# A gated attention and SwiGLU kernel: the product of VectorE's masked key tiles moved to GpSimd

## The chip, the cores and the metric

The kernel runs on one core of one Trainium2 chip. The metric is the device time of one execution in microseconds (us). Before the change it is 769.66 us, the median of three runs (769.5 to 769.75).

The engines of a core work side by side, each on its own queue of instructions in order: TensorE (PE) multiplies matrices into PSUM, ScalarE (ACT) evaluates functions such as the exponential, VectorE (DVE) does elementwise work, GpSimd (POOL) can do elementwise work in SBUF too, and SyncE (SP) starts transfers.

## The reference

An attention block and a SwiGLU block read the same 2048 rows of `x`, and a per-row gate mixes their outputs (bf16; D = 512, 32 heads of 16, F = 1792):

```python
x = A_x
g = sigmoid((x * gate_w).sum(-1, keepdims=True))
q, k, v = split(x @ A_wqkv)                      # 32 heads of 16
p = softmax(einsum("bhqd,bhkd->bhqk", q, k) * 16 ** -0.5)
a = merge(einsum("bhqk,bhkd->bhqd", p, v)) @ A_wo
b = (silu(x @ B_w_gate) * (x @ B_w_up)) @ B_w_down
return g * a + (1 - g) * b
```

The bulk of the elementwise work is the exponential of 32 x 2048 x 2048 scores.

## The kernel before

The scores are computed with keys on the partitions. A *unit* is one block of 512 queries with one group of four heads; there are 4 x 8 = 32 units. A *key tile* is 128 keys of one unit: four heads of 512 queries, so 128x2048 scores. Each unit has 16 key tiles, 512 in all. TensorE makes the scores of a tile (`score`), an engine makes the exponentials in bf16, and TensorE multiplies them with the values and a column of ones (`pv`, accumulating in `o_ps`), one pass of four matmuls for each 128x2048 tile of weights.

Two engines share the exponentials. ScalarE takes the key tiles of a unit from the front, 1024 columns an instruction, from the PSUM tiles `s_t` to `e_all`. VectorE takes tiles from the back of a unit (`v_take`), from PSUM tiles `d_t`, one bank of 512 columns an instruction, and builds an approximation of the exponential out of bit patterns: four evictions (`first` in `emit_d`, line 862) write `y`, a scaled score as a 16-bit integer that read as bf16 is a rough power of two. It then goes on in one of two ways, chosen by `quad` and kept in `groups[n]`:

- four copies (`copy`, line 887): `y` itself and three operations of 128x2048, SBUF to SBUF, that add a constant to the integer; TensorE sums all four, so the tile costs four value passes;
- two copies (`bits` and `product`, lines 895 and 904): one mask keeps the mantissa bits of `y` (line 898), a second keeps sign and exponent (line 901), and a product of `y` and the mantissa mask, read as bf16, makes the second term (line 906). This is two 128x2048 masks and one two-input 128x2048 operation on VectorE, and two value passes.

The results `c_t` lie in six buffers of 128x2048 and a seventh place, which is first a part of `wd_t` and later a part of `kaug`; at most three tiles `y` are in work at a time (`NY`). The feed-forward matmuls, projections and output are cut into pieces that fill TensorE's gaps, and their evictions also go through VectorE. The three PSUM banks of the `m` pools hold `d_t` as well as the pieces.

The order of the instructions on each engine is fixed when the program is built. `ordered` (line 156) chains the instructions of one engine in the order in which the code makes them, so in the profile all VectorE work has the line of that helper, L180, TensorE's L168 and ScalarE's L171. A planner (`Plan`) keeps a clock for each engine, `plan.pe`, `plan.act` and `plan.dve`, adds a fixed price for every instruction, and picks what comes next by these clocks: `fill_dve` orders VectorE's evictions (`d_wait`), masks, copies and products (`vops`) and other work (`owed`); `pv_list` lists the passes whose input is ready by the plan; `v_unit` lets VectorE take another tile if it would be done `LEAD` (in the last unit `LAST`) before ScalarE reaches the end of the unit. On the chip an instruction waits for its inputs by semaphores, but never overtakes the one ahead of it on its engine.

GpSimd only fills constants at the start.

## Time and profile before

| | us |
|---|---|
| median of three runs | 769.66 (769.5 to 769.75) |
| profiled execution | 768.54 |
| its span, first to last instruction | 766.8 |
| TensorE matmul busy | 740.6 (97%) |
| ScalarE busy | 750.8 (98%) |
| VectorE busy | 734.6 (96%) |
| GpSimd busy | 10.6 (1%) |
| granted TensorE clock | 0.999 |

The page of the profile lists the busy time of each engine over the span. The table by stage gives the same for stretches of the span. A group collects the instructions of one engine with the same operation and operands: after the bar come their busy time together, the mean length of one in ns, and the idle time ahead of them with what ended it. In the order of time each row has its start, its length and, in brackets, idle time ahead of it. Lengths are from dispatch to completion, so consecutive rows on one engine can overlap a little; what one more instruction costs is read from start to start.

### The profile page before, as it was taken

To read this page: it belongs to the slowest core of one execution; us is meant where nothing else is said; L and a number is where in the kernel's file an instruction comes from. 1 tells how busy PE (TensorE), PEld (TensorE's weight loads), DVE (VectorE), ACT (ScalarE), POOL (GpSimd) and SP (SyncE) were. 2 spreads that over 40 slices of the span, in tenths; PEclk is the share of its full clock that TensorE was granted. 3 is DMA by queue.
4 is the path that set the end of the run, shared out by engine and by line. 5 is a ranking of instruction groups with operands and counts; after the bars stand their busy time and mean duration, and the time that the engine had idled before them with its cause. 6 is when DMAs were issued, how large, how long until landed. Compare 5 with 4: busy or idle time off the path is not lost.

```text
span 766.8 us, 24169 instructions
## 1 busy us (share of the span) xinstructions
PE 740.6 (97%) x10109; PEld 246.0 (32%) x10109; DVE 734.6 (96%) x1234; ACT 750.8 (98%) x843; POOL 10.6 (1%) x25
## 2 busy tenths in 40 slices
PE   8999999999999999999999999999999999999997
PEld 3333333333333233333333333323333333333332
DVE  7899999999999999999999999999999999999993
ACT  6999999999999999999999999999999999999996
POOL 5000000000000000000000000000000000000000
PEclk9999999999999999999999999999999999999999
DMA  9000313144210013211200130212000232100001
GB/s 222 6 2 15 67 21 78 34 117 87 62 28 13 17 41 78 58 33 28 51 18 24 32 95 21 69 28 56 12 19 17 69 80 56 31 18 7 22 30 35
DMA packets 91029, 34.53 MB, mean 45 GB/s; under 512 B 75488, under 2 KB 90472, under 8 KB 90920
## 3 DMA queue, kind: packets, MB, share of 16 engines
q1 hardware_dynamic: 89192, 32.66, 17.7%
q8 instruction: 79, 1.29, 0.7%
q10 hardware_dynamic: 1728, 0.33, 0.2%
q14 instruction: 30, 0.25, 0.1%
HBM read 21.55 MB, written 2.35 MB: 31 GB/s over the span
## 4 chain that ended last, share of the span: by engine, by line
ACT 48%; PE 27%; DVE 13%; issue 11%; DMA 0%; DVEq 0%; ACTq 0%
ACT e_all L171 45%; DVE c_t L180 9%; PE s_t L168 9%; PE o_ps L168 8%; PE gu L168 5%; ACT th L171 2%; PE dps L168 2%; DVE kaug L180 1%; PE qp L168 1%; DVE mt L180 1%; PE vp L168 1%; PE warm L168 1%; DVE gs L180 1%; DVE osb L180 1%; PE kp L168 0%
## 5 line engine op out<-in xcount | busy, mean ns | idle before, releaser
L171 ACT ACTIVATE e_all<-s_t 128x1024 bf16<-128x1024 f32 x774 | 722.9, 1049 | 3.2 <-PE s_t L168 1.6
L180 DVE TENSOR_SCALAR c_t<-d_t 128x512 uint16<-128x512 f32 x432 | 285.8, 681 | 4.8 <-PE d_t L168 4.5
L168 PE MATMUL s_t<-qx,kaug 32*128 32x512 bf16 (+1 forms) x1224 | 237.6, 385 | 11.6 <-ACT e_all L171 10.2
L168 PE MATMUL o_ps<-e_all,vaug 128*32 128x512 bf16 (+3 forms) x2024 | 170.1, 334 | 0.8 <-ACT e_all L171 0.6
L168 PEld LDWEIGHTS <-kaug 32*128 32x128 bf16 (+1 forms) x2048 | 80.6, 91 | 275.8 <-issue 268.6
L180 DVE TENSOR_SCALAR c_t<-c_t 128x2048 uint16<-128x2048 uint16 x236 | 157.7, 682 | 0.4
L168 PE MATMUL d_t<-qx,kaug 32*128 32x512 bf16 x408 | 153.2, 384 | 0.3 <-DVE qx L180 0.3
L168 PEld LDWEIGHTS <-vaug 128*32 128x32 bf16 x4112 | 101.9, 95 | 131.8 <-issue 94.7
L168 PE MATMUL o_ps<-c_t,vaug 128*32 128x512 bf16 (+3 forms) x1768 | 136.3, 341 | 0.7 <-DVE osb L180 0.6
L168 PE MATMUL gu<-xT,wg 128*32 128x512 bf16 x896 | 71.9, 383 | 0.1
L168 PE MATMUL gu<-xT,wu 128*32 128x512 bf16 x896 | 70.2, 383 | 0.0
L168 PE MATMUL ops<-wd_t,mt 128*32 128x512 bf16 x672 | 58.1, 382 | 0.0
L180 DVE TENSOR_SCALAR kaug<-d_t 128x512 uint16<-128x512 f32 x60 | 40.0, 682 | 0.9 <-PE d_t L168 0.7
L180 DVE SCALAR_TENSOR_TENSOR mt<-gs,gu 128x512 bf16<-128x512 bf16 x56 | 38.1, 680 | 1.6
L180 DVE TENSOR_TENSOR c_t<-c_t 128x2048 bf16<-128x2048 bf16 x32 | 38.8, 1214 | 0.0
L168 PE MATMUL s_t<-q,kaug 32*128 32x512 bf16 (+1 forms) x188 | 36.4, 385 | 2.4 <-ACT e_all L171 2.2
L180 DVE SCALAR_TENSOR_TENSOR gs<-th,gu 128x512 bf16<-128x512 bf16 x56 | 38.0, 678 | 0.1
L171 ACT ACTIVATE th<-gu 128x512 bf16<-128x512 f32 x56 | 35.0, 624 | 0.0
L168 PEld LDWEIGHTS <-mt 128*32 128x32 bf16 (+1 forms) x1037 | 25.0, 95 | 26.2 <-issue 19.6
L180 DVE TENSOR_SCALAR kaug<-c_t 128x2048 uint16<-128x2048 uint16 x46 | 31.3, 680 | 0.0
L180 DVE TENSOR_SCALAR c_t<-kaug 128x2048 uint16<-128x2048 uint16 x42 | 28.1, 683 | 0.0
L168 PEld LDWEIGHTS <-wg 128*32 128x32 bf16 x896 | 18.1, 94 | 25.3 <-issue 21.3
(142 smaller groups left out, 434.1 us busy)
## 6 DMA issues: line engine op xcount, KB each, us to landing
wg<-in_B_w_gate_dram SPq DMA_DIRECT2D x56, 128.0 KB
wu<-in_B_w_up_dram SPq DMA_DIRECT2D x56, 128.0 KB
on<-osb SPq DMA_DIRECT2D x120, 16.0 KB
rb<-rr SPq DMA_DIRECT2D x15, 128.0 KB
wd_t<-in_B_w_down_dram SPq DMA_DIRECT2D x7, 256.0 KB
qx<-qst SPq DMA_DIRECT2D x96, 16.0 KB
qx<-aq SPq DMA_DIRECT2D x96, 16.0 KB
out_dram<-o_t SPq DMA_DIRECT2D x12, 128.0 KB
```

What stands on the lines that cost most here:

```text
L168: return ordered(nc.tensor.matmul(*args, **kw))
L171: ordered(nc.scalar.activation(*args, **kw))
L180: return lambda *a, **kw: ordered(f(*a, **kw))
```

## The change

When VectorE takes a key tile, the planner now asks whether GpSimd has room: the tiles assigned to it and not yet finished by VectorE's masks, at 4.7 us each (`POOL_US`), plus what `plan.pool` is ahead of `plan.dve`, must be below 9 us (`POOL_AHEAD`). If so, the tile takes the two-copy form, and its product is issued on GpSimd instead of VectorE, right after the mantissa mask. The mask of sign and exponent stays on VectorE. If not, `quad` decides as before; in the built program all 38 other tiles of VectorE come out with the four-copy form, so none is left for `product`. A tile for GpSimd keeps its buffer of `y` until both the second mask and the product are done. `LEAD` goes from 8 to 11 us and `LAST` from 6 to 10, and in the count of ScalarE's tiles left the present one is subtracted whole, begun or not. The built program has 94 products on GpSimd; 40 products on VectorE are gone.

```diff
+    gps = Ordered(nc.gpsimd)
...
     class Plan:
-        pe = dve = act = 0.0
+        pe = dve = act = pool = 0.0
...
+    POOL_US, POOL_PE, POOL_AHEAD = 4.7, 0.15, 9
...
             if groups[n] == 2:
-                vops.extend([(0.6, lambda: bits(n, 0, y), ("y", n), n, True), (0.6, lambda: bits(n, 1, y), None, n, True),
-                             (MUL_US, lambda: product(n, h, y), None, n, False)])
+                vops.extend([(0.6, lambda: bits(n, 0, y, h), ("y", n), n, True), (0.6, lambda: bits(n, 1, y, h), None, n, True)])
+                if n in by_pool:
+                    users[h][0] = 2
+                else:
+                    vops.append((MUL_US, lambda: product(n, h, y), None, n, False))
...
+    by_pool = set()
+
+    def bits(n, k, y, i):
         h, c = home()
         if k == 0:
             vec.tensor_scalar(out=c, in0=y, scalar1=0x007F, scalar2=0x3F00, op0=ALU.bitwise_and, op1=ALU.bitwise_or)
             part[n] = (h, c)
+            if n in by_pool:
+                h, c = part.pop(n)
+                gps.tensor_tensor(out=c.bitcast(BF16), in0=y.bitcast(BF16), in1=c.bitcast(BF16), op=ALU.mult)
+                plan.pool = max(plan.pool, plan.dve + 0.1) + POOL_US
+                copies[n, 1] = (c.bitcast(BF16), h)
+                vready.append((plan.pool + POOL_PE, n, 1))
+                drop(i, plan.pool + POOL_PE)
+                y_live[0] -= 1
         else:
+            if n in by_pool:
+                by_pool.remove(n)
+                drop(i, plan.dve + 0.05)
             vec.tensor_scalar(out=c, in0=y, scalar1=0xFF80, scalar2=None, op0=ALU.bitwise_and)
             ready(n, 0, h, c)
...
-    LEAD, LAST = 8.0, 6.0
+    LEAD, LAST = 11.0, 10.0
...
-            left = hi[vu] - (at_ + begun if vu == au else 0)
+            left = hi[vu] - (at_ + 1 if vu == au else 0)
...
-        groups[n] = 2 if quad() else 4
+        if len(by_pool) * POOL_US + max(0.0, plan.pool - plan.dve) < POOL_AHEAD:
+            by_pool.add(n)
+            groups[n] = 2
+        else:
+            groups[n] = 2 if quad() else 4
```

More of the change, by code (lines that the diff above doesn't have):

```diff
@@ L893, in copy @@
             y_live[0] -= 1
-    def bits(n, k, y):
+    by_pool = set()
+    def bits(n, k, y, i):
         h, c = home()
```

## The prediction

> **What bounds the kernel now.** I read the page's busy line first, then the table by stage, then the order of time on VectorE, then the start, the only stretch where GpSimd works.

> ```profile
> PE 740.6 (97%) x10109; PEld 246.0 (32%) x10109; DVE 734.6 (96%) x1234; ACT 750.8 (98%) x843; POOL 10.6 (1%) x25
> ```

> Three engines are full and GpSimd is empty. The table by stage (columns: stretch, its length, busy time and count of TensorE, weight load, VectorE, ScalarE, GpSimd, clock, DMA share, GB/s) shows that this holds nearly to the end:

> ```profile
> 0.00:20.00 20.00, 16.79 (x163) 6.98 (x167) 14.12 (x41) 12.61 (x16) 10.61 (x25) 1.00 0.88 214
> 384.00:480.00 96.00, 93.62 (x1264) 30.71 (x1260) 95.92 (x156) 95.99 (x108) 0.00 (x0) 1.00 0.15 38
> 740.00:767.00 27.00, 22.02 (x275) 8.01 (x273) 13.58 (x25) 20.61 (x24) 0.00 (x0) 0.97 0.08 25
> ```

> Between 20 and 740 us neither ScalarE nor VectorE has more than about 3 us in 96 free. So a gain needs less work on ScalarE, and a loss on VectorE shows in full, but for the little it had free. VectorE's order of time shows what it does (start, length, instruction):

> ```profile
> 400.26 0.68 DVE L180 TENSOR_SCALAR kaug<-c_t 128x2048 uint16<-128x2048 uint16 x1
> 400.86 1.28 DVE L180 TENSOR_SCALAR c_t<-d_t 128x512 uint16<-128x512 f32 x2
> 402.06 1.21 DVE L180 TENSOR_TENSOR c_t<-c_t 128x2048 bf16<-128x2048 bf16 x1
> 403.19 0.68 DVE L180 TENSOR_SCALAR c_t<-d_t 128x512 uint16<-128x512 f32 x1
> ```

> Instructions overlap by about 0.08, so from start to start a 512-column eviction out of PSUM costs 0.60 us, a 2048-column operation inside SBUF also 0.60, and the 2048-column product 1.13. The groups carry the counts (mean length in ns after the comma):

> ```profile
> L171 ACT ACTIVATE e_all<-s_t 128x1024 bf16<-128x1024 f32 x774 | 722.9, 1049 | 3.2 <-PE s_t L168 1.6
> L180 DVE TENSOR_SCALAR c_t<-d_t 128x512 uint16<-128x512 f32 x432 | 285.8, 681 | 4.8 <-PE d_t L168 4.5
> L180 DVE TENSOR_SCALAR c_t<-c_t 128x2048 uint16<-128x2048 uint16 x236 | 157.7, 682 | 0.4
> L180 DVE TENSOR_TENSOR c_t<-c_t 128x2048 bf16<-128x2048 bf16 x32 | 38.8, 1214 | 0.0
> ```

> No row has GpSimd reading two tensors. Its nearest rows are fills:

> ```profile
> L254 POOL MEMSET kaug<- 128x1024 f32 x3 | 2.7, 957 | 0.0
> L522 POOL MEMSET qx<- 128x2048 bf16 x1 | 1.8, 1810 | 0.1
> ```

> 1810 ns for 2048 bf16, 957 for 1024 f32: about 0.9 ns per element and column, whatever its width.

> **The change, part by part.** The counts after are from the listing of the changed program's instructions; durations are the rows above.

> *Tiles and ScalarE.* VectorE's key tiles rise from 125 to 132 (evictions 500 to 528, four each). Seven tiles leave ScalarE: 774 exponentials become 760. Five in a row take 4.72 us of which the last takes its full 1.05, so one costs 0.92 from start to start: 14 x 0.92 = 12.9 us less.

> *TensorE.* 94 VectorE tiles now take the two-copy form (before 40), 38 the four-copy form (before 85). Value passes: before 85x4 + 40x2 + 387 of ScalarE's = 807, after 38x4 + 94x2 + 380 = 720. A second pass adds 0.22 us (0.62 for eight matmuls against 0.40 for four): 19 us less. This lies beside ScalarE; it only means TensorE does not become the bound.

> *VectorE.* 40 products go: -40 x 1.13 = -45.2. SBUF-to-SBUF operations of 2048 columns fall from 335 to 302: -33 x 0.60 = -19.8. Evictions: +28 x 0.60 = +16.8. Sum -48.2; its 734.6 busy become 686.4.

> *GpSimd.* 94 products on an empty queue; the fills of the start are ahead of the first and nothing is behind one but the next. Price of one, from the fill's 0.88 ns per element: one pass over 2048 columns is 1.81, two passes (the two reads) 3.62, three (and the write) 5.43. I take the middle of the last two, 4.5, since both operands must at least be read; 94 x 4.5 = 423 us, so it keeps up. [...]

> *What the product does to VectorE.* This is the term that decides. The fast VectorE forms read SBUF at one rate: 2048 elements in 0.60 us with one input, 4096 in 1.13 with two, 3.4 and 3.6 per ns, against 0.85 out of PSUM. That looks like a read path filled to its limit in both forms. If GpSimd's reads go over part of the same path, the two cannot run together. Lower bound of the cost: nothing (a path of its own). Upper bound: whoever starts first holds the path for its whole instruction. The start shows no collision, but only between writers: VectorE's first fill here runs beside a long GpSimd fill, its second when GpSimd has ended, and both take 0.91.

> ```profile
> 2.65 2.28 POOL L270 MEMSET vaug<- 128x512 bf16 x1
> 3.26 0.91 DVE L254 MEMSET kaug<- 128x1024 f32 x1 [0.16 <-issue]
> ...
> 13.46 0.91 DVE L180 MEMSET kaug<- 128x1024 f32 x1 [0.16 <-issue]
> ```

> I take the upper bound: the row it is nearest to is the one-input form that halves its rate as soon as it must read a second tensor. The price goes by the order of instructions. A product is released by the mantissa mask (L898) that VectorE has just written, some 0.1 us later (an estimate: the overlap of 0.08 and a little). In 76 of 94 cases VectorE's next SBUF-to-SBUF instruction stands one to nine PSUM evictions or the like further on (13 cases one, 29 two, 20 three, 6 four, 5 five, 2 six, 1 nine; 201 in all), and in 70 of these it is the second mask of the same tile (L901). Until then VectorE works beside GpSimd; then it waits for the rest of the product, and everything behind stands still, evictions included. Sum: 76 x 4.6 - 201 x 0.60 = 229 (230 with the one case that does not wait). In the other 18 cases an SBUF operation, mostly that mask, gets in first, the product starts behind it, and the same count from there gives 48. Together 278 us of waiting, 3.0 per product.

> VectorE: 686.4 + 278 + its idle time of before, 766.8 - 734.6 = 32.2 (start, tail, a few waits) = 996.6 us of span. The profiled execution took 768.54 for a span of 766.8, so 1.7 lie around it, and the median of 769.66 is 1.1 above it: 999. TensorE and ScalarE, with about 720 and 738 us of work, run dry behind VectorE: its evictions free the three PSUM banks they queue on. What could come on top: TensorE answering late after each stop; the 11 waits of c_t on d_t total 4.5, 0.41 each, so at most 94 x 0.41 = 39. I take 0, as up to three banks lie filled while VectorE stands. Ends: 278 becomes 199 with a product of 3.62 (920 us), 364 with 5.43 (1085, or 1124 with the 39).

> [...]

> *The planner's other edits.* LEAD 8 to 11, LAST 6 to 10 and the whole tile subtracted for a begun one only shift which tiles VectorE takes and when; they are in the counts. The two-copy form holds its y tile and one of seven buffers until GpSimd is done, 3 to 4 us more; beside VectorE's waiting this delays nothing further. No DMA is added or moved.

> **The rivals.**
> *No collision.* GpSimd reads beside VectorE. Then ScalarE's 14 exponentials decide, VectorE has 48 us to spare, TensorE 19: 769.66 - 12.9 = 757. For it: the fills at the start; against: the read rates. It decides as soon as the waiting per product is under about 0.5 us (48.2 / 94), because that much VectorE has gained.
> *Half a collision.* Both go on at half rate while they meet: GpSimd works 423 of 757 us, 56%; 302 x 0.56 = 169 operations each take 0.60 longer, +101: 686 + 101 + 32 + 3 = 822. A product that TensorE finds late lies here too: the planner places its passes by POOL_US = 4.7; at 5.43 without a collision 94 x 0.73 = 69 on 757, 826. So does a cheap product under full exclusion, below 3.62.
> *Cancelling out.* Exclusion with a product of one pass, 1.81: 50 us of waiting, 686 + 50 + 32 + 3 = 771, no change.

> **How the numbers follow.** Full exclusion 0.69 (its own range 910 to 1125); half a collision, late or cheap products 0.13 (785 to 910); no collision 0.16 (750 to 765); cancelling out 0.02. The predicted time is the first one's, 999. The range 785 to 1125 takes in the first two, 0.82 less a little at the ends. A measurement of this kernel tells about 0.2% (1.5 us) from no change. Faster 0.16, same 0.02, slower 0.82.

> **What the changed profile would show.** Right: 2048-column masks whose mean is far above 0.68 us, or idle time of VectorE in front of them while a GpSimd product runs; VectorE near its span counting waits, ScalarE down to some 75%, evictions out of PSUM still at 0.68; the GpSimd product 3.6 to 5.4. Wrong: masks at 0.68 beside running products (then ScalarE stays at 98% and the time falls), or a product so long that TensorE waits for it.

## The result and the profile after

The changed kernel takes 1010.23 us (median of four runs, 1008.21 to 1016.52) against 769.68 before: the ratio is 1.314, 95% interval 1.3079 to 1.32. The profiled execution has a span of 1014.7 us.

The busy line of the changed kernel's page:

```profile
PE 836.6 (82%) x9681; PEld 242.4 (24%) x9681; DVE 905.9 (89%) x1189; ACT 762.5 (75%) x829; POOL 398.0 (39%) x119
```

ScalarE fell from 98% to 75% of the span, and VectorE, with fewer instructions than before (1189 for 1234), is busy 171 us longer. Its groups and GpSimd's say where:

```profile
L180 POOL TENSOR_TENSOR c_t<-c_t 128x2048 bf16<-128x2048 bf16 x68 | 279.9, 4116 | 432.2 <-DVE c_t L180 368.4
L180 DVE TENSOR_SCALAR c_t<-d_t 128x512 uint16<-128x512 f32 x448 | 297.0, 681 | 42.4 <-PE d_t L168 39.2
L180 DVE TENSOR_SCALAR c_t<-c_t 128x2048 uint16<-128x2048 uint16 x213 | 273.9, 1295 | 3.7 <-PE o_ps L168 2.2
L180 DVE TENSOR_SCALAR kaug<-c_t 128x2048 uint16<-128x2048 uint16 x42 | 55.1, 1312 | 0.1
L180 DVE TENSOR_TENSOR on<-on,rb 128x512 bf16<-128x512 bf16 x15 | 15.0, 1022 | 0.0
```

Evictions out of PSUM still take 681 ns. The 2048-column operations inside SBUF, 682 ns before, now average 1295 and 1312. A two-input operation of 512 columns, `on<-on,rb`, went from 416 to 1022 ns; its line before:

```profile
L180 DVE TENSOR_TENSOR on<-on,rb 128x512 bf16<-128x512 bf16 x15 | 5.8, 416 | 0.0
```

A stopped instruction is not shown as idle time here: the wait is inside its length, and VectorE looks busier. VectorE's rows in the order of time, and GpSimd's from the same stretch (three dots stand for rows left out):

```profile
496.64 1.27 DVE L180 TENSOR_SCALAR c_t<-d_t 128x512 uint16<-128x512 f32 x2
497.84 3.65 DVE L180 TENSOR_SCALAR kaug<-c_t 128x2048 uint16<-128x2048 uint16 x1
501.42 0.68 DVE L180 TENSOR_SCALAR c_t<-d_t 128x512 uint16<-128x512 f32 x1
...
525.67 0.73 DVE L180 TENSOR_SCALAR o_t<-ops,omg 128x512 bf16<-128x512 f32 x1
526.33 0.67 DVE L180 TENSOR_SCALAR c_t<-d_t 128x512 uint16<-128x512 f32 x1
526.93 2.99 DVE L180 TENSOR_SCALAR c_t<-c_t 128x2048 uint16<-128x2048 uint16 x1
529.85 0.68 DVE L180 TENSOR_SCALAR c_t<-d_t 128x512 uint16<-128x512 f32 x1
```

```profile
496.89 4.06 POOL L180 TENSOR_TENSOR c_t<-c_t 128x2048 bf16<-128x2048 bf16 x1 [8.56 <-DVE c_t L180]
...
520.15 4.45 POOL L180 TENSOR_TENSOR c_t<-kaug,c_t 128x2048 bf16<-128x2048 bf16 x1 [12.65 <-DVE c_t L180]
525.32 4.05 POOL L180 TENSOR_TENSOR c_t<-c_t 128x2048 bf16<-128x2048 bf16 x1 [0.72 <-DVE c_t L180]
```

The product of 525.32 ends at 529.37. The PSUM evictions next to it keep their 0.67 and 0.68 us; the mask dispatched at 526.93 ends at 529.92, 0.55 us after the product. An unhindered mask takes 0.68, so nearly all of its work lies behind the product's end. The product of 496.89 ends at 500.95, the mask that it stops at 501.49, again 0.54 later. Over the whole run 88 instructions of VectorE are lengthened, and 80 of them end 0.55 or 0.56 us after a product, however long they had waited.

Added up as count times mean above the length of before, the five 2048-column groups lost 184 us (213 x 0.613, 42 x 0.630, 35 x 0.560, 10 x 0.465, 2 x 1.127), and the smaller operations inside SBUF 24 more: 208 us of VectorE's 905.9 are stops. Its idle time is 1014.7 - 905.9 = 109 us, where before it was 32.

### The profile page after: what moved, and what is told of

It is laid out like the page before. It is cut to its first block, busy times and chain, and to the rows that moved or that the text cites. A ratio compares the mean times of both kernels' runs of the same rounds, so it can differ in the third digit from the quotient of the medians.

```text
span 1014.7 us, 23458 instructions
## 1 busy us (share of the span) xinstructions
PE 836.6 (82%) x9681; PEld 242.4 (24%) x9681; DVE 905.9 (89%) x1189; ACT 762.5 (75%) x829; POOL 398.0 (39%) x119
## 3 DMA queue, kind: packets, MB, share of 16 engines
HBM read 21.55 MB, written 2.35 MB: 24 GB/s over the span
## 4 chain that ended last, share of the span: by engine, by line
DVE 52%; PE 36%; ACT 6%; issue 4%; DMA 0%; SPq 0%; DVEq 0%; ACTq 0%
DVE c_t L180 37%; PE s_t L168 11%; PE o_ps L168 9%; ACT e_all L171 6%; DVE kaug L180 6%; PE gu L168 6%; PE ops L168 3%; DVE mt L180 2%; PE qp L168 2%; DVE on L180 1%; PE d_t L168 1%; DVE aq L180 1%; PE vp L168 1%; DVE gs L180 1%; DVE wd_t L180 1%
## 5 line engine op out<-in xcount | busy, mean ns | idle before, releaser
L171 ACT ACTIVATE e_all<-s_t 128x1024 bf16<-128x1024 f32 x760 | 730.7, 1031 | 237.8 <-PE d_t L168 121.3
L180 POOL TENSOR_TENSOR c_t<-c_t 128x2048 bf16<-128x2048 bf16 x68 | 279.9, 4116 | 432.2 <-DVE c_t L180 368.4
L180 DVE TENSOR_SCALAR c_t<-d_t 128x512 uint16<-128x512 f32 x448 | 297.0, 681 | 42.4 <-PE d_t L168 39.2
L180 DVE TENSOR_SCALAR c_t<-c_t 128x2048 uint16<-128x2048 uint16 x213 | 273.9, 1295 | 3.7 <-PE o_ps L168 2.2
L168 PE MATMUL s_t<-qx,kaug 32*128 32x512 bf16 (+1 forms) x1204 | 259.1, 428 | 11.1 <-ACT e_all L171 10.5
L168 PE MATMUL d_t<-qx,kaug 32*128 32x512 bf16 x428 | 174.0, 426 | 22.9 <-DVE c_t L180 14.5
L168 PE MATMUL o_ps<-c_t,vaug 128*32 128x512 bf16 (+3 forms) x1496 | 122.5, 359 | 82.1 <-DVE c_t L180 78.7
L168 PE MATMUL o_ps<-e_all,vaug 128*32 128x512 bf16 (+3 forms) x1952 | 179.9, 369 | 0.0
L168 PEld LDWEIGHTS <-vaug 128*32 128x32 bf16 x3684 | 94.4, 99 | 259.6 <-issue 229.5
L168 PEld LDWEIGHTS <-kaug 32*128 32x128 bf16 (+1 forms) x2048 | 79.1, 93 | 319.9 <-issue 315.3
L168 PE MATMUL gu<-xT,wu 128*32 128x512 bf16 x896 | 82.5, 435 | 10.2 <-DVE kaug L180 4.1
L180 POOL TENSOR_TENSOR c_t<-kaug,c_t 128x2048 bf16<-128x2048 bf16 x13 | 54.7, 4207 | 86.1 <-DVE c_t L180 86.1
L168 PE MATMUL gu<-xT,wg 128*32 128x512 bf16 x896 | 82.6, 428 | 6.5 <-DVE c_t L180 3.4
L168 PE MATMUL ops<-wd_t,mt 128*32 128x512 bf16 x672 | 65.4, 437 | 0.0
L180 POOL TENSOR_TENSOR kaug<-c_t,kaug 128x2048 bf16<-128x2048 bf16 x9 | 36.6, 4063 | 64.2 <-DVE kaug L180 54.3
L180 DVE TENSOR_SCALAR kaug<-c_t 128x2048 uint16<-128x2048 uint16 x42 | 55.1, 1312 | 0.1
L180 DVE TENSOR_SCALAR kaug<-d_t 128x512 uint16<-128x512 f32 x64 | 42.9, 682 | 6.1 <-PE d_t L168 5.9
L180 DVE SCALAR_TENSOR_TENSOR mt<-gs,gu 128x512 bf16<-128x512 bf16 x56 | 38.2, 681 | 7.7 <-PE gu L168 5.0
L180 DVE TENSOR_SCALAR c_t<-kaug 128x2048 uint16<-128x2048 uint16 x35 | 42.9, 1242 | 0.6 <-PE o_ps L168 0.4
L180 DVE SCALAR_TENSOR_TENSOR gs<-th,gu 128x512 bf16<-128x512 bf16 x56 | 37.9, 677 | 2.8 <-ACT th L171 2.3
L168 PE MATMUL s_t<-q,kaug 32*128 32x512 bf16 (+1 forms) x184 | 38.1, 410 | 1.5 <-ACT e_all L171 1.1
L168 PE MATMUL d_t<-q,kaug 32*128 32x512 bf16 x72 | 29.8, 430 | 9.8 <-DVE c_t L180 6.9
```

The source lines that it names most:

```text
L168: return ordered(nc.tensor.matmul(*args, **kw))
L171: ordered(nc.scalar.activation(*args, **kw))
L180: return lambda *a, **kw: ordered(f(*a, **kw))
```

## The experiments

### Without the product

```diff
-                gps.tensor_tensor(out=c.bitcast(BF16), in0=y.bitcast(BF16), in1=c.bitcast(BF16), op=ALU.mult)
```

> The 94 GpSimd products are left out (the second pass of such a tile multiplies the bare mantissa mask), all else stands as in the changed kernel. Theory of the collision: VectorE does not wait any more, its masks are back at 0.68 us, ScalarE bounds again, 757 us (750 to 765), granted clock near 1.0. Rival, that the planner's other edits and the other mix of tiles cost the time: it stays above 950.

Measured: 755.84 us, ratio to the kernel before 0.9827 (0.9812 to 0.9841). Granted clock 1.0. The page's busy line and the mask's group:

```profile
PE 724.6 (96%) x9681; PEld 235.2 (31%) x9681; DVE 692.7 (92%) x1189; ACT 738.0 (98%) x829; POOL 10.6 (1%) x25
```

```profile
L180 DVE TENSOR_SCALAR c_t<-c_t 128x2048 uint16<-128x2048 uint16 x213 | 143.9, 686 | 3.1 <-PE o_ps L168 2.2
```

The same order without the product is 254 us faster than the changed kernel, and the masks are back at 686 ns. The new mix of tiles, with the product left out, is worth 1.7%; the product on GpSimd costs 254 us, 2.7 us for each of the 94. ScalarE, 98% busy, bounds this run, and VectorE idles 62 us behind it.

### The products in the same places, on VectorE

```diff
-                gps.tensor_tensor(out=c.bitcast(BF16), in0=y.bitcast(BF16), in1=c.bitcast(BF16), op=ALU.mult)
+                vec.tensor_tensor(out=c.bitcast(BF16), in0=y.bitcast(BF16), in1=c.bitcast(BF16), op=ALU.mult)
```

> The 94 products stand in the same places but on VectorE: 94 x 1.13 = 106 us more work for it, 686 + 106 + 32 idle + 3 = 827 us (815 to 850), masks at 0.68. Theory: faster than the changed kernel by some 180 us, although VectorE does more. Rival, that the product's place in the order is what costs: 1010 and above.

Measured: 870.27 us (864.88 to 872.96), ratio 1.1305 (1.1264 to 1.1347). VectorE does some 106 us more work than in the changed kernel, and the kernel is 140 us faster: the place in the order is not what costs. The expected 827 was 43 too low, and the time lies outside the expected 815 to 850. VectorE is busy 804.9 us of a span of 862.6, where 792 were counted, and it idles 58 us, not 32. The waits fit an order that was made for a VectorE without these products: ScalarE and TensorE find their inputs late, and then VectorE finds its own late. That the order is the cause is not shown:

```profile
ACT e_all L171 <- PE s_t L168: 53.2, 72, 2.2
ACT e_all L171 <- PE d_t L168: 37.6, 56, 1.4
PE d_t L168 <- DVE c_t L180: 22.2, 33, 1.2
```

(The waits: who waited, for whom, us in total, times, longest.)

### The planner's three edits alone

```diff
-    LEAD, LAST = 8.0, 6.0
+    LEAD, LAST = 11.0, 10.0
...
-            left = hi[vu] - (at_ + begun if vu == au else 0)
+            left = hi[vu] - (at_ + 1 if vu == au else 0)
```

> The kernel before with the three edits of the planner (LEAD, LAST, the whole tile subtracted) and no GpSimd: 780 exponentials for 774, 6 x 0.92 = 5.5 us more, 775 us (771 to 781). If these edits carried the loss: above 900.

Measured: 775.17 us, ratio 1.007 (1.0054 to 1.0087), as the six more exponentials price it. These edits do not carry the loss.

### Another form of the second mask

```diff
+    probe = const.tile([P, 1], F32, name="probe")
...
-            if n in by_pool:
-                by_pool.remove(n)
-                drop(i, plan.dve + 0.05)
-            vec.tensor_scalar(out=c, in0=y, scalar1=0xFF80, scalar2=None, op0=ALU.bitwise_and)
-            ready(n, 0, h, c)
+            by_pool.remove(n)
+            vec.tensor_reduce(out=probe[:, 0:1], in_=y[:, 0:1024].bitcast(BF16), axis=AX.X, op=ALU.max)
+            drop(h, plan.dve)
+            ready(n, 0, i, y)
```

> The second mask of each GpSimd tile becomes a slower VectorE operation that also reads y in SBUF but in a one-element-per-step form, a maximum over 1024 columns (1.15 us from start to start for 0.60, 90 times, 50 us more work); the first value pass reads y itself. Theory that only VectorE's fast one-input forms and its two-input forms wait for GpSimd: the waits fall from about 200 us to some 60, 1010 - 120 = 890 us (860 to 905), the maximum stays at 1.2 us beside running products. Rival, that any VectorE read of SBUF waits: 1040 to 1080.

Measured: 877.3 us, ratio 1.1416 (1.1388 to 1.1445): 133 us faster than the changed kernel with some 50 us more work on VectorE. Its stops add up to 63 us, where some 60 were expected. VectorE's and GpSimd's order of time:

```profile
506.65 1.21 DVE L180 TENSOR_REDUCE probe<-kaug 128x1 f32<-128x1024 bf16 x1
...
508.75 1.15 DVE L180 TENSOR_TENSOR rn<-rd 128x128 bf16<-128x128 f32 x1
...
519.44 1.21 DVE L180 TENSOR_REDUCE probe<-c_t 128x1 f32<-128x1024 bf16 x1
520.57 2.87 DVE L180 TENSOR_TENSOR on<-on,rb 128x512 bf16<-128x512 bf16 x1
```

```profile
505.68 4.08 POOL L180 TENSOR_TENSOR c_t<-kaug,c_t 128x2048 bf16<-128x2048 bf16 x1 [6.29 <-DVE c_t L180]
519.10 4.06 POOL L180 TENSOR_TENSOR c_t<-c_t 128x2048 bf16<-128x2048 bf16 x1 [9.34 <-PE s_t L168]
```

Both maxima run inside a product's time and take 1.21 us. So do 66 of the 90, and over all 90 the longest takes 1.216. They read `y` in SBUF, the same tile that GpSimd reads. The two-input operations behind them wait: 1.15 us for one of 0.29 before, ending 0.14 us after its product, and 2.87 for one of 0.42, ending 0.28 after. So in this run it is neither the tile nor SBUF reading as such, but the form of VectorE's instruction. Writing to SBUF as such is not it either: the evictions write there beside a product and keep their 0.68.

### Fills in place of products

```diff
-                gps.tensor_tensor(out=c.bitcast(BF16), in0=y.bitcast(BF16), in1=c.bitcast(BF16), op=ALU.mult)
+                gps.memset(c.bitcast(BF16), 1.0)
+                gps.memset(c.bitcast(BF16), 1.0)
```

> Each GpSimd product is replaced by two fills of the same 128x2048 tile, which write and read nothing (2 x 1.81 us, against 4.06 us of a product). Theory that the path is held by any GpSimd instruction against VectorE's fast one-input form: masks wait for fills, some 91 us in all by the order of instructions, 686 + 91 + 32 + 3, and some 40 that VectorE idles as in the run with the products on VectorE: 850 us (790 to 880). Rival, that only GpSimd's reads collide: masks at 0.68, 757 us.

Measured: 852.1 us, ratio 1.1073 (1.1058 to 1.1088). GpSimd reads nothing here, and the masks still wait:

```profile
L180 POOL MEMSET c_t<- 128x2048 bf16 x166 | 331.8, 2000 | 394.5 <-DVE c_t L180 362.7 <-PE gu L168 12.1 <-PE d_t L168 6.7
L180 DVE TENSOR_SCALAR c_t<-c_t 128x2048 uint16<-128x2048 uint16 x213 | 199.7, 947 | 4.1 <-PE o_ps L168 2.7
```

A 2048-column operation averages 947 ns in place of 686 without GpSimd, and VectorE's stops add up to 92 us, as the count by order had it (91). The fill's mean, 2000 ns, is also longer than the 1810 of the one at the start, which had no such operation beside it. The 188 fills fall into two groups: 110 take 1.8 us and 78 take 2.2 to 2.35, and each of the 78 began while a one-input operation of VectorE inside SBUF, such as a mask, was under way. The stop works both ways. The two-input operation is not stopped here: the seven `on<-on,rb` that began during a fill took 0.41 to 0.42 us, as in the kernel before.

### Half a product

```diff
-                gps.tensor_tensor(out=c.bitcast(BF16), in0=y.bitcast(BF16), in1=c.bitcast(BF16), op=ALU.mult)
+                gps.tensor_tensor(out=c.bitcast(BF16)[:, 0:1024], in0=y.bitcast(BF16)[:, 0:1024],
+                                  in1=c.bitcast(BF16)[:, 0:1024], op=ALU.mult)
```

> The GpSimd product covers only the first 1024 of the 2048 columns, about 2.06 us in place of 4.06; the other half of the mantissa mask goes on unmultiplied. Theory that a mask waits for what is left of the product: waits by the order of instructions 66 us in place of 230, 686 + 66 + 35 + 25 = 812 us (780 to 840). Rival, a fixed cost for each meeting of the two engines: 94 x 2.7 us stays, about 1010.

Measured: 822.09 us, ratio 1.0706 (1.0676 to 1.0735).

```profile
L180 POOL TENSOR_TENSOR c_t<-c_t 128x1024 bf16<-128x1024 bf16 x68 | 148.2, 2180 | 427.9 <-DVE c_t L180 356.1 <-PE d_t L168 30.6 <-PE o_ps L168 13.9
```

Half the product costs 66 us over no product (822.1 - 755.8), the whole one 254; VectorE's stops are 65 us and 208. The price is no fixed cost for each meeting, nor proportional to the length. This fits the count by the order of instructions that stands behind the expected 812: the first two microseconds of a product are mostly covered by evictions, the next two are not.

### A planner that knows the collision

```diff
-    POOL_US, POOL_PE, POOL_AHEAD = 4.7, 0.15, 9
+    POOL_US, POOL_PE, POOL_AHEAD = 4.2, 0.15, 0.1
...
-        spend_v(cost, 0.0, key)
+        spend_v(cost, plan.pool, key)
...
-            fit = bool(vops) and vops[0][3] // KT <= closed + AHEAD and c_ready() <= now
+            fit = bool(vops) and vops[0][3] // KT <= closed + AHEAD and max(c_ready(), plan.pool) <= now
...
-                        + [c_ready()] * bool(vops and vops[0][3] // KT <= closed + AHEAD))
+                        + [max(c_ready(), plan.pool)] * bool(vops and vops[0][3] // KT <= closed + AHEAD))
...
-    LEAD, LAST = 11.0, 10.0
+    LEAD, LAST = 5, 5
...
-            left = hi[vu] - (at_ + 1 if vu == au else 0)
+            left = hi[vu] - (at_ + begun if vu == au else 0)
```

> The planner knows the collision: it puts no 2048-column operation of VectorE behind a product until the product is done by its clock, prices the product at 4.2 us, hands GpSimd one tile at a time, and LEAD and LAST are 5. 39 products on GpSimd, 15 on VectorE, 770 exponentials for the 774 of the kernel before. If all collisions are avoided 4 x 0.92 = 3.7 us faster than before, 766 us; by the order of instructions about 33 us of waiting are left, of which VectorE's spare time takes most: 766 to 790. Rival, that any GpSimd product costs: 39 x 2.6 = 100 us, 860.

Measured: 781.12 us, ratio 1.0154 (1.0139 to 1.0169), far from the rival's 860 but 1.5% slower than the kernel before. With 39 products on GpSimd most of the stops are gone (the mask group's mean is 702 ns); 16 instructions are still stopped, seven masks among them, for 21 us in all. What is left:

```profile
L180 DVE TENSOR_SCALAR c_t<-c_t 128x2048 uint16<-128x2048 uint16 x236 | 162.1, 702 | 0.1
L180 DVE TENSOR_SCALAR c_t<-d_t 128x512 uint16<-128x512 f32 x432 | 288.5, 685 | 20.0 <-PE d_t L168 16.6 <-PE s_t L168 1.5
```

Part of the stop has become idle time: VectorE stands 20.0 us in front of `c_t<-d_t`, where the kernel before stood 4.8, and it idles 46.5 us in all, not 32. With the stops that are left, this eats the four exponentials saved and some 12 us more. The collision can mostly be ordered around. In this order the 39 products do not gain; that there is not enough other work at the right moment is the likely reason, and whether another order would gain is not shown.

### LEAD alone

```diff
-    LEAD, LAST = 8.0, 6.0
+    LEAD, LAST = 6.0, 5.0
```

> The kernel before with LEAD 6 and LAST 5 only, no GpSimd: 772 exponentials for 774, 1.8 us less on ScalarE, 768 us (766 to 771). It tells what of the run with the planner that knows the collision is due to LEAD alone.

Measured: 769.38 us, ratio 1.0 (0.9991 to 1.0009). Earlier limits alone neither gain nor cost, so the 1.5% of the run above are not theirs alone; LEAD 5 itself was not tried without GpSimd.

### More matmuls for TensorE's clock

The changed kernel's granted clock is 0.879 of full speed in the mean, and its matmuls of `d_t` average 426 ns for 384. Before it was 0.999. The group before and after:

```profile
L168 PE MATMUL d_t<-qx,kaug 32*128 32x512 bf16 x408 | 153.2, 384 | 0.3 <-DVE qx L180 0.3
L168 PE MATMUL d_t<-qx,kaug 32*128 32x512 bf16 x428 | 174.0, 426 | 22.9 <-DVE c_t L180 14.5
```

The run adds matmuls on zero weights behind a product, where the accumulation in progress allows it:

```diff
+                if closed in o_of and 0 < pvs[closed] and not cut and pv_left(closed) > 1 and (closed or pvs[0] != KT // 2):
+                    for j in list(range(4)) * 6:
+                        mm(o_of[closed][32 * j:32 * j + 16, :], lhsT=vaug[:, 0, G * 4 * VC:], rhs=xT[:, 0, 0:QBW],
+                           start=False, stop=False, tile_position=(0, 32 * j), skip_group_check=True)
```

> The changed kernel with 24 more matmuls on zero weights (six sets of four, 6 x 0.22 = 1.3 us) in TensorE's order behind 64 of the 94 products, 83 us of work in all, to see what the lower granted clock of the changed kernel (0.879) costs. Theory that TensorE's clock is a by-product of its gaps and VectorE's waits decide: the clock rises, the time stays within 1000 to 1025 us. Rival, that the lower clock carries part of the loss: with the clock above 0.95 the time falls to 960 to 990.

Measured: 1002.82 us (996.61 to 1007.16), ratio 1.3008 (1.2962 to 1.3053), clock 0.931. The median stays where the first theory has it, and the added TensorE work, some 83 us by the estimate above, did not make the kernel longer. But the clock came back by less than half, short of the 0.95 of the rival, and the time is some 7 us lower, so the run does not decide between the two. VectorE's stops fell from 208 to 161 us while its idle time rose from 109 to 145 (1005.2 - 859.8): the two kinds of waiting replace each other in part.

The executions of one and the same program point to more than 7 us. The changed kernel took 1008.21 us at a clock of 0.897 and 1016.52 at 0.879; with the added matmuls it took 996.61 at 0.949 and 1007.16 at 0.931. Carried on as a straight line to the full clock, this would be 40 to 56 us of the 254, an estimate far outside of what was measured. What a full clock would give is left open.

### The runs side by side

| GpSimd's work beside VectorE | us | mean of `c_t<-c_t` 128x2048, ns | VectorE's stops, us | VectorE idle, us | clock |
|---|---|---|---|---|---|
| none (product left out) | 755.8 | 686 | 0 | 62 | 1.000 |
| 94 half products, 2.18 us | 822.1 | 866 | 65 | 63 | 0.979 |
| 188 fills, 2.00 us | 852.1 | 947 | 92 | 68 | 0.977 |
| none (94 products on VectorE) | 870.3 | 685 | 0 | 58 | 0.988 |
| 90 products, reduction for the second mask | 877.3 | 812 | 63 | 72 | 0.958 |
| 94 products (the change) | 1010.2 | 1295 | 208 | 109 | 0.879 |

Stops are what VectorE's instructions are longer than the same ones without GpSimd beside them. Idle is the span less VectorE's busy time.

## Why the prediction was right

*What bounds it, and ScalarE's gain.* Right. Without a collision the sum gave 757; the run without the product took 755.84. ScalarE did lose its 14 exponentials; the gain exists and is paid for elsewhere.

*VectorE's own work.* 686.4 forecast, 692.7 measured where GpSimd is idle.

*The price of a product.* 4.5 taken between 3.62 and 5.43; its median is 4.064 us, so mis-sized by a tenth. It lies midway between two passes at a fill's price, 3.62, and the 4.5.

*Full exclusion.* Right in kind: the upper bound is what happens. The stopped instruction does its work after the product has ended, whichever tile it works on, in the forms named (the one-input 2048-column form, a two-input operation), while evictions (0.68 us) and the reduction (1.21) keep their length. It holds the other way round too: 17 of the 94 products take 4.11 to 4.45 us for a median of 4.06, and each of these began while a mask or a two-input operation of VectorE was under way. In the trace the one that started first runs its usual length and the other is the longer: the 16 masks under way at the start of such a product took 0.68 to 0.69 us, and a mask that came second took up to 4.5 us.

The reason given for it, a read path filled to its limit, holds only in part. A fill reads nothing and still stops the masks, so for the one-input form GpSimd's reading is not needed. For the two-input operation a stop shows only where GpSimd reads: beside a product `on<-on,rb` took up to 4.28 us, beside a fill it kept its 0.41 to 0.42.

*The size of the waiting.* 278 us forecast, 208 measured. The same count with 4.06 us for the product gives 76 x 4.16 - 201 x 0.60 + 1 = 197, and about 40 for the other 18 cases (48 - 18 x 0.44): 237. That the rest is spent on evictions that VectorE finds late while a product runs, so that less of it is left when the mask comes, is argued, not shown.

*What could come on top.* This is the term that failed: 0 taken, at most 39 thought possible. VectorE's idle time rose from 32 to 109, by 77. The reason given, three filled banks, does not hold: the waits of `c_t` on `d_t` alone went from 4.5 to 39.2. With the products on VectorE and no GpSimd work VectorE idles 58 us already, so 26 of the 77 need no collision, only an order planned for another VectorE. That is argued, not shown. The other 51 come with the longer stops and the slower clock, which the runs do not separate. The trace speaks for a large part of the clock: without the first and last 30 us, VectorE idles 44 us in the 239 us at half clock, and 39 in the 716 at full clock. At the rate of the full clock the 239 would hold 13, so some 31 of the 51 lie there (an estimate).

The forecast span of 996.6 missed the measured 1014.7 by 18. The waiting was 70 too much, the idle time 77 too little, and VectorE's own work 12 too little (905.9 - 208 = 698 for 686): the mis-sizings cancelled. That is luck, and the 999 is nearer to 1010 than its terms deserve.

*The rivals.* No collision: refuted by the lengths, and its price confirmed by the run that removes the product. Half a collision: VectorE's stopped masks do not go on at half rate. They finish 0.55 us after the product, whether they met it early or late; at half rate, one that met it early would be through before its end. A product that TensorE finds late: no wait of TensorE on GpSimd is among its listed waits; it waits for VectorE (`o_ps` on `c_t`, 78.7 us).

## What to carry to other kernels

An idle engine is not free capacity until a run has shown what its work does to the engine beside it. Before moving work to GpSimd beside a VectorE that is as full as here, count VectorE's instructions in SBUF of the forms that were stopped in these runs (the one-input masks and copies, 0.68 us for 2048 columns, and two-input operations, 0.42 us for `on<-on,rb`), see how far behind the hand-over the next one stands, and charge the product's length (4.06 us here) less the work in between for each. If the sum is above what VectorE saves, the move loses. Here 208 us of stops stood against 48 us of work saved.

## What the runs showed of the hardware that was not expected

A stop by the other engine does not appear as idle time but as a longer instruction: 0.68 us became up to 4.5 us, and VectorE's busy time rose by 171 us while its work fell. A busy share alone would have been read as more work.

```profile
595.61:599.02 3.41, 2.25 (x25) 0.62 (x21) 3.38 (x6) 3.08 (x4) 0.00 (x0) 1.00 0.00 0
599.02:602.43 3.41, 3.41 (x30) 0.66 (x26) 2.56 (x5) 1.40 (x2) 0.00 (x0) 0.50 0.02 5
```

Cut into such stretches of 3.41 us, the changed kernel's trace has half clock behind every full-clock stretch in which TensorE was busy for less than 0.54 of it, and behind none in which it was busy for more than 0.63. With the products on VectorE half clock also followed the stretch shown above, in which it was busy for 0.66 (2.25 of 3.41), so the share alone does not decide.
